# Score matmuls of a chunked linear-attention kernel: from two 64-column strips of the array to four of 32

## The chip, the cores and the metric

The kernel runs on one core of one Trainium2 chip. A core has a matrix engine (TensorE, PE in the profile; its weight loads are listed apart as PEld), a vector engine (VectorE, DVE), a scalar engine (ScalarE, ACT), a general one (GpSimd, POOL), a queue engine (SyncE, SP) and 16 DMA engines. Matmul results land in PSUM, eight banks of 2 KB per partition; everything else on the chip lies in SBUF. The metric is the device time of one execution in microseconds, lower is better; the time of a kernel is the median of its runs.

## The reference, cut to what matters

Two blocks follow each other. The first is a gated linear recurrence, per batch and head, over 768 tokens with head size 48; the second puts its output through four experts and adds them up with weights.

```python
# batch 4, heads 8, tokens S = 768, head size 48
for t in range(S):
    state = alpha[:, :, t, :, None] * state + np.einsum('bhd,bhe->bhde', k[:, :, t], v[:, :, t])
    y[:, :, t] = np.einsum('bhd,bhde->bhe', q[:, :, t], state)
x = y.transpose(0, 2, 1, 3).reshape(3072, 384)
p = domain_probs / (domain_probs.sum(-1, keepdims=True) + 1e-09)
for e in range(4):                       # w1[e]: 384 x 1024, w2[e]: 1024 x 384
    out += p[:, e:e + 1] * (np.maximum(x @ w1[e], 0.0) @ w2[e])
```

All of it is float32.

## The kernel before, in words

**Units.** The tokens are cut into chunks of 128. A unit is one chunk of one batch, 24 in all (6 chunks x 4 batches). Its eight heads lie in four pairs; a head is padded from 48 to 64 rows, so that a pair fills the 128 rows of the array. A unit makes the output of its 128 tokens out of the state that the chunk before left, and out of the products of its own keys and queries.

**Levels.** A key s and a later query t of one chunk get a score that carries the gates between them. The kernel orders the pairs (s, t) by the size at which they part in a binary tree over the 128 tokens: at level m (1, 2, 4, ... 64; `LEVELS`, index li 0 to 6) the keys are the lower halves and the queries the upper halves of blocks of 2m tokens. Query and key tiles are multiplied by gates from one level to the next (`next_q`, line 490, `next_k`, line 499); `copy_q` (line 480) copies the 64 queries of the upper halves into a tile `qb` in which the two heads of a pair stand side by side, each in its own 64 rows, with zeros elsewhere. `qb` has four buffers, handed round by the deque `free`.

**Scores.** For levels 1 to 32 (li 0 to 5) `products` (line 509) makes eight matmuls, one for each pair of heads and each half s of the keys: 64 key columns as weights, 2 x 32 query columns streamed, the result in 64 of the 128 PSUM partitions. Two such matmuls, for s = 0 and 1, stand side by side in the array, in two strips of 64 columns. In a half, the result of 64 keys x 32 queries holds all blocks of that half, and only the entries inside a block count. `take` (line 519) picks them out with a mask of 0 and 1: a predicated copy on DVE of 128 x 256 elements (8 heads x 32 queries) into `near`, which has 128 x 8 x 64 elements and starts as a diagonal of the terms with s = t (line 539). Level 64 (li 6) needs no mask: four groups of matmuls (line 569) write `far`, and ACT copies it to its place in `lat` (line 582). Later ACT copies the two 64 x 64 diagonal blocks of `near` into `lat` (line 586), and `result` (line 594) multiplies `lat` by the values and adds the state's part, in four strips of 32 columns (line 608).

**PSUM.** Score tiles have the tag "sc" with two buffers of one bank. Levels 0 to 3 take two tiles of two levels each (line 542), levels 4 and 5 a third (line 564), `far` a fourth.

**Precision.** These matmuls are plain float32: the profile lists each as two records of matmul and two of weight load. The matmuls of the experts are float32r (one record), three of them for each product, because operands are split into a rounded and a rest part; only the first group of units runs them in plain float32.

**The order of the work.** Everything that PE does is issued in the order of the program; PE executes it in that order, except that matmuls in different strips of the array go on side by side. The experts' matmuls (`up`, line 660; `down`, line 723) carry the program. `attention(u)` (line 422) is a generator with 17 steps, parted by `yield`; `deal` (line 810) gives each step of each unit a due time on a clock that counts only the experts' work (`cost`, line 804), and `advance` (line 858) runs the due steps between two of the experts' matmuls. Steps counted from 0: 0 to 2 turn alpha, k, q; 3 to 5 do levels 0 to 2 of `copy_q`, `next_q`, `next_k`; 6 copies level 3 and sets up `near`; 7 issues the products of levels 0 to 3 together and takes levels 0 and 1; 8 takes levels 2 and 3; 9 and 10 prepare levels 5 and 6; 11 issues the products of levels 64, 16 and 32 together and takes levels 16 and 32; 12 copies `far`; 13 copies the diagonal of `near`; 14 and 15 turn the keys and make the result; 16 renews the state. Two units are under way at a time, and for many units step 7 is put right behind step 15 of the unit before (`TOGETHER`, line 131). The first unit has a function of its own (`first_unit`, line 239), with matmuls of 64 rows x 64 columns and 32 streamed columns in four tiles of the array at once (line 295).

Of the kernel before, what the change touches and what calls it, by code (L numbers as in the profile page):

```python
# [20 lines left out]
def kernel(  # L21
# [35 lines left out]
    mask_np = np.concatenate([mask_np.reshape(P, -1), j == np.arange(HALF)[None, :]], 1).astype(np.uint8)  # L57
    used = (np.arange(P)[:, None] % HD < D)
    ident_np = np.concatenate([np.eye(P), np.tile(np.eye(HALF), (2, 1)), used], 1).astype(np.float32)
# [8 lines left out]
    ident_all = const.tile([P, P + HALF + 1], F32, name="ident")  # L68
    ident = ident_all[:, :P]
    masks_all = const.tile([P, 6 * QUAD + HALF], U8, name="masks")  # L70
    masks = masks_all[:, :6 * QUAD].rearrange("p (l n) -> p l n", n=QUAD)
    NBLK = B * NCB
    p_all = const.tile([P, NBLK, E], F32, name="p_all")
    tot = const.tile([P, NBLK], F32, name="tot")

    near = const.tile([P, H, HALF], F32, name="near")
    lat = const.tile([P, H, P], F32, name="lat")

    sts = [const.tile([P, NP, 2, D], F32, name=f"st{b}") for b in range(B)]
# [30 lines left out]
    free = deque(blocks)  # L110
# [128 lines left out]
    def first_unit(fill, other):  # L239
# [17 lines left out]
        rows = [slice(HD * i, HD * (i + 1)) for i in range(2)]  # L257
# [44 lines left out]
        def take(li, outs):  # L302
            for i in range(2):
                to = diag[:, NP * i:NP * (i + 1)]
                if li < 0:
                    nc.vector.copy_predicated(
                        to, masks_all[:, 6 * QUAD:].unsqueeze(1).broadcast_to([P, NP, HALF]), outs[i])
# [114 lines left out]
    def attention(u):  # L422
        cb, b = units[u]
# [18 lines left out]
        yield  # L442
        KT = keys()
        if u >= in_runs:
            nc.scalar.activation(out=AT, in_=AT, func=ACT.Copy, scale=ident_all[:, P + HALF:])  # L445
            turn("k", KT)
        else:
            nc.scalar.copy(out=KT, in_=turned(pair(rk)))
# [50 lines left out]
        def next_k(li):  # L499
            m = LEVELS[li]  # L500
            old = new = halves(KTs[li], m)
            if li + 1 < len(LEVELS):
# [3 lines left out]
            nc.vector.tensor_mul(new[:, :, :, 0, :], old[:, :, :, 0, :],  # L506
                                 spread(halved(decs[li])[:, :, :, 1], m))

        def products(li, out):

            for p in range(NP):
                for s in range(2):
                    nc.tensor.matmul(  # L513
                        out[HALF * s:HALF * (s + 1), 2 * p:2 * p + 2, :],
                        lhsT=KTs[li][:, p, HALF * s:HALF * (s + 1)],
                        rhs=qbs[li][:, p, :, QUAD * s:QUAD * (s + 1)], start=True, stop=True)
            free.append(qbs[li])

        def take(li, scores):
            m = LEVELS[li]  # L520
            nb = HALF // (2 * m)
            mk = masks[:, li, :].rearrange("p (b r) -> p b r", r=m)
            nc.vector.copy_predicated(  # L523
                near.rearrange("p a (b two r) -> p a b two r", two=2, r=m)[:, :, :, 1, :],
                mk.unsqueeze(1).broadcast_to([P, H, nb, m]),
                scores.rearrange("p a (b r) -> p a b r", r=m))

        def scores():
            return ps.tile([P, 2, H, QUAD], F32, name="sc", tag="sc")


        for li in range(3):
# [3 lines left out]
            yield  # L536
        copy_q(3)

        nc.vector.tensor_mul(near, ident_all[:, P:P + HALF].unsqueeze(1).broadcast_to([P, H, HALF]),
                             dot.unsqueeze(2).broadcast_to([P, H, HALF]))  # L540
        yield
        banks = [scores() for _ in range(2)]
        for li in range(4):
            products(li, banks[li // 2][:, li % 2])
        next_q(3)
        next_k(3)
        take(0, banks[0][:, 0])
        take(1, banks[0][:, 1])
        yield
        copy_q(4)  # L550
        next_q(4)
        next_k(4)
        take(2, banks[1][:, 0])
        take(3, banks[1][:, 1])
        yield
        copy_q(5)
        next_q(5)
# [4 lines left out]
            next_q(6)  # L562
        yield
        bank = scores()
        far = ps.tile([P, NP // 2, 2, HALF], F32, name="far", tag="sc")

        for r in range(NP // 2):
            for s in range(2):
                nc.tensor.matmul(far[HALF * s:HALF * (s + 1), r],  # L569
                                 lhsT=KTs[6][:, 2 * r + s, :HALF], rhs=qbs[6][:, 2 * r + s],  # L570
                                 start=True, stop=True)
        for li in (4, 5):
            products(li, bank[:, li - 4])
        free.append(qbs[6])
        take(4, bank[:, 0])
        take(5, bank[:, 1])
        next_k(6)
        yield
        parts = lat.rearrange("p (r s i) c -> p r s i c", s=2, i=2)
        for s in range(2):  # L580
            rows = slice(HALF * s, HALF * (s + 1))
            nc.scalar.copy(out=parts[:HALF, :, s, :, HALF:], in_=far[rows])
        yield
        for s in range(2):
            rows = slice(HALF * s, HALF * (s + 1))
            nc.scalar.copy(out=lat[rows, :, rows], in_=near[rows])
        KT = KTs[-1]
        yield
# [275 lines left out]
    with tc.manual_schedule():  # L864
        nc.scalar.dma_start(out=ident_all, in_=nc.inline_tensor(ident_np, name="ident_c").ap())
        nc.scalar.dma_start(out=masks_all, in_=nc.inline_tensor(mask_np, name="masks_c").ap())
        nc.gpsimd.memset(sts[B - 1], 0.0)
        for nm in "akq":
            for r in (early[nm], apart[nm]):
                nc.gpsimd.memset(r[:, :, D:], 0.0)  # L870
        nc.gpsimd.memset(lat[HALF:, :, :HALF], 0.0)
        for t in values + blocks:
            nc.gpsimd.memset(t, 0.0)
        for t in sts[:-1]:
            nc.gpsimd.memset(t, 0.0)
# [72 lines left out]
```

## Time and profile before

| what | value |
|---|---|
| median of 3 runs | 1011.13 us (1010.61 to 1011.39) |
| the profiled execution's own time | 1010.73 us |
| its span in the trace | 1009.0 us |
| PE matmul busy | 994.1 us, 99% |
| PE weight load busy | 885.8 us, 88% |
| DVE busy | 547.0 us, 54% |
| ACT busy | 426.0 us, 42% |
| POOL busy | 36.1 us, 4% |
| granted PE clock | 1.0 |
| score matmuls, line 513 | 2208 records, 73.7 us busy |
| predicated copies, line 523 | 138 of 128 x 256, 536 ns each |

A line of the profile names the line of the kernel, the engine, the operation, the tiles (out<-in), the shape and a count; "128*64 128x64" at a matmul means 128 rows and 64 columns of the array in use and 64 columns streamed. Busy time is the union of the records, so that overlapping matmuls are not counted twice; the mean of one record is its latency, not the pace at which records follow each other. "Issue" as a reason for idle time means that the profile shows nothing that the engine waited for.

### The profile page before, as it was taken

The page shows a single profiled execution, that of the slowest core. Times are in us where ns is not written, and L with a number is a line of the kernel's source. Part 1 is how long each engine was busy: PE and PEld are TensorE (multiplying, and loading weights), DVE is VectorE, ACT ScalarE, POOL GpSimd, SP SyncE. Part 2 cuts the span into 40 slices and gives each one's busy share as a digit, 9 for nine tenths or more (in the row PEclk, how much of TensorE's full clock was granted, in tenths as well). Part 3 has the DMA queues.
Part 4 walks back from the last instruction along what each step waited for, and adds up shares of the span by engine and source line. Part 5 has one row for each costly group of instructions (what it writes and reads, how often), then busy time and mean ns, then how long its engine had stood idle before and what let it go on. Part 6 is the DMA issues. An engine that isn't in the chain of part 4 may idle for free.

```text
span 1009.0 us, 20864 instructions
## 1 busy us (share of the span) xinstructions
PE 994.1 (99%) x8564; PEld 885.8 (88%) x8564; DVE 547.0 (54%) x1178; ACT 426.0 (42%) x936; POOL 36.1 (4%) x79
## 2 busy tenths in 40 slices
PE   8899999999999999999999999999999999999998
PEld 7777778988988889889899899898898989999998
DVE  5677757366676555666645645756676521222222
ACT  5786666354463552533533514445443432111111
POOL 2000001000000000000000000000000000000000
PEclk9999999999999999999999999999999999999999
DMA  9696788284776683854945828748656405151511
GB/s 210 220 291 201 239 285 306 71 325 118 269 228 210 216 232 124 276 196 150 316 146 178 293 100 247 252 123 277 218 159 253 155 8 196 55 206 45 206 60 32
DMA packets 155118, 194.12 MB, mean 192 GB/s; under 512 B 95216, under 2 KB 131440, under 8 KB 155024
## 3 DMA queue, kind: packets, MB, share of 16 engines
q1 hardware_dynamic: 148560, 162.97, 51.2%
q0 software_dynamic: 6016, 29.49, 7.5%
q8 instruction: 68, 1.11, 0.5%
q10 hardware_dynamic: 448, 0.33, 0.1%
q14 instruction: 26, 0.21, 0.1%
HBM read 162.87 MB, written 29.88 MB: 191 GB/s over the span
## 4 chain that ended last, share of the span: by engine, by line
PE 92%; DVE 3%; ACT 3%; issue 1%; DMA 1%; SPq 0%; DVEq 0%; ACTq 0%
PE ops L764 40%; PE one L695 35%; PE sc L513 6%; PE yps L608 3%; PE one L689 3%; PE tp L236 2%; PE sps L639 1%; PE far L569 1%; ACT qb L487 1%; DVE w L210 1%; DMA sk<-in_k_dram 1%; DVE near L523 1%; DMA w<-kept 0%; ACT KT L505 0%; DVE QT L494 0%
## 5 line engine op out<-in xcount | busy, mean ns | idle before, releaser
L764 PE MATMUL ops<-w,hT 128*128 128x384 f32 x2112 | 380.6, 338 | 0.1
L764 PEld LDWEIGHTS ops<-w,hT 128*128 128x128 f32 x2112 | 364.4, 188 | 4.0 <-issue 0.8
L695 PE MATMUL one<-xT,w 128*128 128x512 f32 x1440 | 340.4, 394 | 0.0
L695 PEld LDWEIGHTS one<-xT,w 128*128 128x128 f32 x1440 | 268.3, 188 | 56.9
L697 ACT ACTIVATE hT<-one 128x512 fp32r<-128x512 f32 (+1 forms) x192 | 108.0, 562 | 302.5 <-PE one L695 301.7
L720 DVE SCALAR_TENSOR_TENSOR hT<-one,hT 128x512 fp32r<-128x512 f32 (+1 forms) x192 | 121.8, 642 | 117.5 <-ACT hT L697 117.4
L487 ACT COPY qb<-QT 64x256 f32<-64x256 f32 x322 | 131.2, 407 | 68.0 <-DVE QT L494 36.4
L494 DVE TENSOR_TENSOR QT<-QT,AT 128x256 f32<-128x256 f32 x158 | 66.8, 423 | 103.3 <-ACT qb L487 102.6
L790 DVE SCALAR_TENSOR_TENSOR acc<-ops,p_all,acc 128x384 f32<-128x384 f32 x66 | 38.1, 612 | 91.8 <-PE ops L764 91.8
L523 DVE COPY_PREDICATED near<-masks,sc 128x256 f32<-128x256 uint8 x138 | 74.0, 536 | 20.6 <-PE sc L513 18.1
L513 PEld LDWEIGHTS sc<-qb,KT 128*64 128x64 f32 x2208 | 69.5, 138 | 7.0 <-issue 5.3
L513 PE MATMUL sc<-qb,KT 128*64 128x64 f32 x2208 | 73.7, 223 | 1.3 <-ACT qb L487 1.2
L506 DVE TENSOR_TENSOR KT<-KT,AT 128x256 f32<-128x256 f32 x161 | 67.2, 418 | 3.1 <-PE tp L236 3.1
L505 ACT COPY KT<-KT 128x256 f32<-128x256 f32 x138 | 57.5, 417 | 3.4
L689 PE MATMUL one<-xT,raw 128*128 128x256 f32 (+1 forms) x240 | 46.0, 340 | 0.4 <-ACT xT L406 0.4
L764 PE MATMUL ops<-raw,hT 128*128 128x384 f32 x128 | 45.5, 492 | 0.0
L689 PEld LDWEIGHTS one<-xT,raw 128*128 128x128 f32 x240 | 37.9, 191 | 4.9 <-ACT xT L406 0.6
L496 DVE TENSOR_TENSOR AT<-AT 128x256 f32<-128x256 f32 (+1 forms) x138 | 39.2, 284 | 4.7
L799 POOL DMA_DIRECT2D out_dram<-acc x22 | 11.8, 541 | 680.2 <-DVE acc L790 680.2
L445 ACT ACTIVATE AT<-AT,ident 128x512 f32<-128x512 f32 x14 | 10.2, 726 | 60.8 <-DVE AT L434 59.9
L695 PE MATMUL one<-raw,w 128*128 128x256 f32 x288 | 34.6, 279 | 0.0
L695 PEld LDWEIGHTS one<-raw,w 128*128 128x128 f32 x288 | 34.4, 188 | 0.0
(110 smaller groups left out, 631.6 us busy)
## 6 DMA issues: line engine op xcount, KB each, us to landing
w<-kept SPq DMA_DIRECT2D x144, 768.0 KB, 7.2
kept<-w POOLq DMA_DIRECT2D x32, 768.0 KB, 6.3
raw<-in_moe_w_dram SPq DMA_DIRECT2D x48, 384.0 KB, 6.7
rv<-in_v_dram SPq DMA_DIRECT2D x24, 192.0 KB, 2.9
out_dram<-acc POOLq DMA_DIRECT2D x22, 192.0 KB, 2.4
rk<-in_k_dram SPq DMA_DIRECT2D x14, 192.0 KB, 3.2
rq<-in_q_dram SPq DMA_DIRECT2D x14, 192.0 KB, 8.6
sa<-in_alpha_dram SPq DMA_DIRECT2D x28, 88.0 KB, 2.1
```

What stands on the lines that cost most here:

```text
L487: nc.scalar.copy(out=qb[rows, :, i, :].rearrange("p a (b r) -> p a b r", r=m), in_=qv[rows])
L494: nc.vector.tensor_mul(qv, qv, spread(dv[:, :, :, 0], m))
L496: nc.vector.tensor_mul(dec, dv[:, :, :, 0], dv[:, :, :, 1])
L505: nc.scalar.copy(out=new[:, :, :, 1, :], in_=old[:, :, :, 1, :])
L506: nc.vector.tensor_mul(new[:, :, :, 0, :], old[:, :, :, 0, :], spread(halved(decs[li])[:, :, :, 1], m))
L513: nc.tensor.matmul(out[HALF * s:HALF * (s + 1), 2 * p:2 * p + 2, :], lhsT=KTs[li][:, p, HALF * s:HALF * (s + 1)], rhs=qbs[li][:, p, :, QUA ...
L523: nc.vector.copy_predicated(near.rearrange("p a (b two r) -> p a b two r", two=2, r=m)[:, :, :, 1, :], mk.unsqueeze(1).broadcast_to([P, H, ...
L689: nc.tensor.matmul(one, lhsT=w[:, kc], rhs=xTs[gi][:, 0, kc, lo:hi], start=(kc == 0), stop=(kc == KC - 1))
L695: nc.tensor.matmul(one, lhsT=w[:, of_w, kc], rhs=x_part(gi, of_x)[:, kc, :n], start=k == 0, stop=k == len(turns) - 1)
L697: nc.scalar.activation(out=parts[0], in_=one, func=ACT.Relu)
L720: nc.vector.scalar_tensor_tensor(out=low, in0=x, scalar=0.0, in1=top.bitcast(F32), op0=ALU.max, op1=ALU.subtract)
L764: nc.tensor.matmul(sums[slot], lhsT=h, rhs=w, start=(n == begins[slot]), stop=(n == ends[slot]))
```

## The change

Levels 1 to 16 (li 0 to 4) go from two strips of 64 keys to four strips of 32: a level is now 16 matmuls with 32 weight columns and 2 x 16 streamed columns, in place of eight with 64 and 2 x 32. `near` shrinks from 64 to 32 columns per head, the masks (`strip_masks`) and the copies of `take` from 32 to 16 queries per head. Four levels fit in one bank, so step 7 takes one score tile and step 11 one.

Level 32 (li 5) leaves `products` and `take`: inside a half of 64 tokens it is one full block of 32 keys x 32 queries, so it needs no mask. Its eight matmuls use 32 weight columns each; a strip is given to one half s of one of two pairs of heads (`odd`), so that two pairs are done at once. ACT copies the result from PSUM into `lat` in four pieces, in step 12, behind the two copies of `far`. `cross` and `far` are parts of the bank that holds level 16. In step 11 the order is now level 64, level 16, level 32. In step 13 the diagonal is copied in four pieces of 32 x 32 per head in place of two of 64 x 64. All of `lat` is zeroed at the start, in place of a quarter.

```diff
+    NSTRIP = P // QUAD
+    HQ = QUAD // 2
+    strip_np = np.stack([(js // (2 * m) == n[:, :HQ] // m) & (js % (2 * m) < m) for m in LEVELS[:5]], 1)
...
-    near = const.tile([P, H, HALF], F32, name="near")
+    near = const.tile([P, H, QUAD], F32, name="near")
...
+        strips = [slice(QUAD * j, QUAD * (j + 1)) for j in range(NSTRIP)]
+
         def products(li, out):
-
             for p in range(NP):
-                for s in range(2):
-                    nc.tensor.matmul(
-                        out[HALF * s:HALF * (s + 1), 2 * p:2 * p + 2, :],
-                        lhsT=KTs[li][:, p, HALF * s:HALF * (s + 1)],
-                        rhs=qbs[li][:, p, :, QUAD * s:QUAD * (s + 1)], start=True, stop=True)
+                for j, rows in enumerate(strips):
+                    nc.tensor.matmul(out[rows, 2 * p:2 * p + 2, :], lhsT=KTs[li][:, p, rows],
+                                     rhs=qbs[li][:, p, :, HQ * j:HQ * (j + 1)], start=True, stop=True)
             free.append(qbs[li])
...
         def scores():
-            return ps.tile([P, 2, H, QUAD], F32, name="sc", tag="sc")
+            return ps.tile([P, 4, H, HQ], F32, name="sc", tag="sc")
...
-        banks = [scores() for _ in range(2)]
+        bank = scores()
         for li in range(4):
-            products(li, banks[li // 2][:, li % 2])
+            products(li, bank[:, li])
...
         bank = scores()
-        far = ps.tile([P, NP // 2, 2, HALF], F32, name="far", tag="sc")
-
+        cross = bank[:, 1].rearrange("p a n -> p (a n)").rearrange("p (r i n) -> p r i n", r=NP // 2, i=2)
+        far = bank[:, 2:].rearrange("p l a n -> p (l a n)").rearrange("p (r i n) -> p r i n", r=NP // 2, i=2)
...
-        for li in (4, 5):
-            products(li, bank[:, li - 4])
         free.append(qbs[6])
+        products(4, bank[:, 0])
+        for r in range(NP // 2):
+            for j, rows in enumerate(strips):
+                odd, s = divmod(j, 2)
+                nc.tensor.matmul(cross[rows, r], lhsT=KTs[5][:, 2 * r + odd, strips[2 * s]],
+                                 rhs=qbs[5][:, 2 * r + odd, :, QUAD * s:QUAD * (s + 1)], start=True, stop=True)
+        free.append(qbs[5])
         take(4, bank[:, 0])
-        take(5, bank[:, 1])
         next_k(6)
         yield
...
             nc.scalar.copy(out=parts[:HALF, :, s, :, HALF:], in_=far[rows])
-        yield
-        for s in range(2):
-            rows = slice(HALF * s, HALF * (s + 1))
+        for j, rows in enumerate(strips):
+            odd, s = divmod(j, 2)
+            nc.scalar.copy(out=parts[strips[2 * s], :, odd, :, strips[2 * s + 1]], in_=cross[rows])
+        yield
+        for rows in strips:
             nc.scalar.copy(out=lat[rows, :, rows], in_=near[rows])
...
-        nc.gpsimd.memset(lat[HALF:, :, :HALF], 0.0)
+        nc.gpsimd.memset(lat, 0.0)
```

More of the change, by code (lines that the diff above doesn't have):

```diff
@@ L57 @@
     mask_np = np.concatenate([mask_np.reshape(P, -1), j == np.arange(HALF)[None, :]], 1).astype(np.uint8)
+    NSTRIP = P // QUAD
+    HQ = QUAD // 2
+    js = np.arange(P)[:, None] % QUAD
+    strip_np = np.stack([(js // (2 * m) == n[:, :HQ] // m) & (js % (2 * m) < m) for m in LEVELS[:5]], 1)
+    mask_np = np.concatenate([mask_np, strip_np.reshape(P, -1)], 1).astype(np.uint8)
     used = (np.arange(P)[:, None] % HD < D)
-    ident_np = np.concatenate([np.eye(P), np.tile(np.eye(HALF), (2, 1)), used], 1).astype(np.float32)
+    ident_np = np.concatenate([np.eye(P), np.tile(np.eye(QUAD), (NSTRIP, 1)), used], 1).astype(np.float32)
     const = ctx.enter_context(tc.tile_pool(name="const", bufs=1))
@@ L66 @@
     ps = ctx.enter_context(tc.tile_pool(name="ps", bufs=2, space=bass.MemoryType.PSUM))
-    ident_all = const.tile([P, P + HALF + 1], F32, name="ident")
+    ident_all = const.tile([P, P + QUAD + 1], F32, name="ident")
     ident = ident_all[:, :P]
-    masks_all = const.tile([P, 6 * QUAD + HALF], U8, name="masks")
+    masks_all = const.tile([P, 6 * QUAD + HALF + 5 * HQ], U8, name="masks")
     masks = masks_all[:, :6 * QUAD].rearrange("p (l n) -> p l n", n=QUAD)
+    same = masks_all[:, 6 * QUAD:6 * QUAD + HALF]
+    strip_masks = masks_all[:, 6 * QUAD + HALF:].rearrange("p (l n) -> p l n", n=HQ)
     NBLK = B * NCB
@@ L306, in take @@
                     nc.vector.copy_predicated(
-                        to, masks_all[:, 6 * QUAD:].unsqueeze(1).broadcast_to([P, NP, HALF]), outs[i])
+                        to, same.unsqueeze(1).broadcast_to([P, NP, HALF]), outs[i])
                     continue
@@ L444, in attention @@
         if u >= in_runs:
-            nc.scalar.activation(out=AT, in_=AT, func=ACT.Copy, scale=ident_all[:, P + HALF:])
+            nc.scalar.activation(out=AT, in_=AT, func=ACT.Copy, scale=ident_all[:, P + QUAD:])
             turn("k", KT)
@@ L520, in take @@
             m = LEVELS[li]
-            nb = HALF // (2 * m)
-            mk = masks[:, li, :].rearrange("p (b r) -> p b r", r=m)
+            nb = QUAD // (2 * m)
+            mk = strip_masks[:, li, :].rearrange("p (b r) -> p b r", r=m)
             nc.vector.copy_predicated(
@@ L537, in attention @@
         copy_q(3)
-        nc.vector.tensor_mul(near, ident_all[:, P:P + HALF].unsqueeze(1).broadcast_to([P, H, HALF]),
-                             dot.unsqueeze(2).broadcast_to([P, H, HALF]))
+        nc.vector.tensor_mul(near, ident_all[:, P:P + QUAD].unsqueeze(1).broadcast_to([P, H, QUAD]),
+                             dot.unsqueeze(2).broadcast_to([P, H, QUAD]))
         yield
-        banks = [scores() for _ in range(2)]
+        bank = scores()
         for li in range(4):
-            products(li, banks[li // 2][:, li % 2])
+            products(li, bank[:, li])
         next_q(3)
         next_k(3)
-        take(0, banks[0][:, 0])
-        take(1, banks[0][:, 1])
+        take(0, bank[:, 0])
+        take(1, bank[:, 1])
         yield
@@ L552, in attention @@
         next_k(4)
-        take(2, banks[1][:, 0])
-        take(3, banks[1][:, 1])
+        take(2, bank[:, 2])
+        take(3, bank[:, 3])
         yield
```

## The prediction

> **What bounds the kernel now.** First the engines' shares and the chain that ended last, then the stretches, then the rows of the score matmuls.
>
> ```profile
> PE 994.1 (99%) x8564; PEld 885.8 (88%) x8564; DVE 547.0 (54%) x1178; ACT 426.0 (42%) x936; POOL 36.1 (4%) x79
> ...
> PE 92%; DVE 3%; ACT 3%; issue 1%; DMA 1%; SPq 0%; DVEq 0%; ACTq 0%
> PE ops L764 40%; PE one L695 35%; PE sc L513 6%; PE yps L608 3%; PE one L689 3%; PE tp L236 2%; PE sps L639 1%; PE far L569 1%; ACT qb L487 1%; DVE w L210 1%; DMA sk<-in_k_dram 1%; DVE near L523 1%; DMA w<-kept 0%; ACT KT L505 0%; DVE QT L494 0%
> ```
>
> PE is the bound, and the score matmuls (L513) are 6% of the chain. By stretches (columns: stretch, its length, busy time of each engine with its records, clock, DMA share, GB/s):
>
> ```profile
> 20.00:130.00 110.00, 104.64 (x1071) 83.14 (x1072) 75.08 (x173) 78.13 (x186) 7.59 (x14) 1.00 0.74 232
> 130.00:350.00 220.00, 219.04 (x1912) 191.68 (x1912) 138.41 (x297) 109.36 (x233) 13.27 (x27) 1.00 0.68 232
> 350.00:620.00 270.00, 270.00 (x2342) 242.85 (x2340) 154.65 (x326) 108.88 (x235) 2.14 (x4) 1.00 0.64 205
> 620.00:830.00 210.00, 210.00 (x1873) 189.56 (x1873) 126.41 (x272) 91.30 (x202) 4.30 (x8) 1.00 0.56 181
> ```
>
> From 130 us to 830 us PE has no idle time worth naming, DVE and ACT are half idle, and the DMA engines have room. So PE time taken out there shortens the span one for one; before 130 us some of it is lost to waits. One unit's score matmuls, in the timeline of PE alone (start, time to the last end, line, records):
>
> ```profile
> 379.26 0.40 PE L608 MATMUL yps<-lat,rv 128*32 128x128 f32 x8
> 379.59 2.08 PE L513 MATMUL sc<-qb,KT 128*64 128x64 f32 x64
> 381.61 0.45 PE L764 MATMUL ops<-w,hT 128*128 128x384 f32 x1
> ...
> 394.11 0.62 PE L569 MATMUL far<-qb,KT 128*64 128x128 f32 x8
> 394.56 1.10 PE L513 MATMUL sc<-qb,KT 128*64 128x64 f32 x32
> 395.59 0.45 PE L764 MATMUL ops<-w,hT 128*128 128x384 f32 x1
> ```
>
> From its first matmul to the next line's first, levels 0 to 3 take 2.015 us and levels 4 and 5 1.031 us, 3.05 us a unit, 70 us for 23 units (the first has its own function, untouched).
>
> **The pace of small matmuls.** In the trace's single starts the records of one strip follow each other every 58.3 ns in L513, with the other strip 6.6 ns beside it. Which side sets this?
>
> ```profile
> L639 PE MATMUL sps<-rv,AT x208: 222/243/275, 44.5 to 704.2; 128*64 128x48 f32 x56, 128*128 128x96 f32 x48
> ...
> L404 PE MATMUL y<-w,rv x64: 216/219/243, 17.7 to 20.1; 64*32 64x64 f32 x32, 128*32 128x64 f32 x32
> ...
> L295 PE MATMUL sc<-w,w x96: 186/219/240, 9.8 to 16.3; 64*64 64x32 f32 x96
> ```
>
> With 64 weight columns the step is 58.3 ns for 32 (L295), 48 (L639) and 64 streamed columns alike; with 128 weight columns and 96 streamed it is 111.7 ns (L639's other form); with 32 weight columns and 64 streamed it falls to 55.9 ns (L404), with 128 streamed to 109 ns (L608). So the weight load sets it at 64 and 128 columns, 53.4 ns per 64: at 32 columns 58.3 - 26.7 = 31.6 ns. The stream sets L404 and L608, 53.1 ns per 64 columns: at 32 columns 55.9 - 26.6 = 29.3 ns. The later holds: 31.6 ns for a record in each of four strips, 7.9 ns a record. That is an extrapolation; no row has 32 weight columns with 32 streamed. Its support: at a burst's start, L608's second load in a strip begins 29 ns after the first, L513's 55 ns.
>
> The queue must deliver one record per 7.9 ns. Usually it runs some 16 records ahead; where it had run dry (46.3 us) it passed 20 records in 151 ns, 7.6 each, and at 70.2 us 12 in 88 ns, 7.3 each. That just suffices. The 51 ns semaphore events, two a unit at L513, are covered now by 16 records at 29 ns; then by 16 at 7.9, 126 ns. I put 0.05 us a unit on them.
>
> **PE, part by part.** Levels 0 to 3: 64 matmuls are 128 records, 32 groups of four at 31.6 ns, 1.01 us, plus 0.14 us of ends (now 0.15 us): 1.15 us for 2.015, -0.865. Level 4: 8 groups, 0.25 us. Level 5: 8 matmuls are 16 records with 64 streamed columns, four groups at L404's 55.9 ns, 0.22 us. Ends 0.15 us. L569 before them has 64-column strips, and a change of strip width drains the array: from L608 (32) to L513 (64) the last start to the next first is 203 ns, against 109 within L608; that is 0.1 us more here. Sum 0.72 for 1.031, -0.31. Where L608 stands right before levels 0 to 3, 15 times, the drain goes away: 15 x 0.094 = -1.4 us.
>
> Unit 1 (29 to 40 us) I count at nothing: there the chain runs over ACT and DVE (L487, L494, L523), so what PE saves becomes waiting. Beside it DVE gets shorter by four takes and `near`, about 0.9 us, and ACT longer by up to 1.5 us before the result; net between -1 and +1 us, taken as 0. Sum: 22 x (0.865 + 0.31 - 0.05) + 1.4 = 26.1 us off.
>
> **DVE.** Per unit six copies of 536 ns become five of 128 x 128. L311 has that shape, 382 ns (scores) and 274 ns: 1.9 us at the dearer for 3.2. Setting up `near`, 682 ns at 128 x 512, becomes about 423 ns (L494's 128 x 256). That is 1.6 us less, 36 us in all, hidden under PE: no gain, no cost.
>
> **ACT.** Two copies of 64 x 512 at 616 ns become four of 32 x 256, between 363 (L582) and 407 ns (L487): 1.23 to 1.6 us. Four copies of 32 x 128 are added, nearest L271's 128 x 128 at 298 ns: 1.2 us. Some 1.5 us more a unit, 35 us in all, ACT at 46%. In step 12 six copies hold ACT about 1.9 us instead of 0.73. Queued behind them are the experts' relu (L697) and the other unit's `qb` copies; who waits then is PE, for a score or hidden tile. The relu's tile has three more buffers, each some 2 us of PE; steps lie 3 us or more apart. I take 0; uncovered, it is up to 35 us.
>
> **PSUM.** One tile a step instead of two: step 11 no longer holds both buffers. I take 0; the nearest waits, DVE for L513, are not PE's.
>
> **Start and DMA.** POOL's zeroing of `lat` quadruples in area: 523 ns for 64 x 512 is about 1.05 us for 128 x 1024. The value tile (L873) behind it is what SP waits for at 3.31 us; all of SP's later loads move by 0.5 us. Unit 1's alpha would land near 10.1 us and is used at 10.9, the first weights near 16 and 20.7: hidden; uncovered 0.5 us. The instruction queue moved 1.11 MB for 17128 PE records; 3680 more are 0.24 MB, 15 fetches of about 1 us beside the rest. No other queue gets or loses a step.
>
> So 1010.7 - 26.1 = 984.6 us for the profiled execution; it lies 0.4 us under the median, which gives 985.0.
>
> **The rivals.** With r ns a record, a unit's two bursts are 160 r + 591 ns, against 3046 and some 60 of drain.
>
> *The queue does not keep up.* At 7.3 to 7.6 ns the margin is thin. At r = 10 a unit saves 0.91 us, at 12 0.59: 991 to 999 us. Against it are the two catches above; for it, that they are the only ones.
>
> *A 32-column stream costs as much as a 64-column one.* L404's 55.9 ns per four is r = 14.0, L295's 58.3 is 14.6: 0.27 or 0.18 us a unit, 1005 to 1007 us. For it: L295's median latency is 219 ns, L404's with 64 columns too. Against it: the first records of a burst, which wait for their weights, last 240 ns (L295, 32 columns), 257 (L639, 48) and 270 (L513, 64), on a straight line. [...]
>
> [...]
>
> *Slower: ACT's extra copies end on PE.* Place: steps 12 and 13, ahead of the next unit's `qb` copies. Price: 1.5 us x 23 = 35 us against 26 gained, 1019 us; it decides from 1.1 us a unit on PE. For it: at 99.6 us a burst already stands 1.46 us for ACT's `qb`. Against: from 350 to 620 us PE never waits, ACT is 40% busy, and DVE, ahead of it in that chain, gets 1.6 us shorter.
>
> **How the numbers follow.** Chances: the forecast 0.64 (980 to 989: r from 7.3, unit 1 gaining 1 us and no event cost, to 9.3); the queue 0.10; the stream's floor 0.13; no change, r from 15 to 16.4, 0.03; slower 0.10, of it ACT 0.08 and the floor for all strips 0.01. Changes under 0.2% (2 us) can't be told from none, the runs spread by 0.8 us. Faster 0.87, same 0.03, slower 0.10. The range takes the forecast and the queue (0.74) and reaches into the stream's floor: 979 to 1006.
>
> **What would show it.** L513's starts in a strip 31 to 33 ns apart and its first burst 1.1 to 1.2 us long; the second near 0.6 us behind a gap of 0.2; copies of L523's successor under 0.4 us; ACT near 460 us, DVE near 511; PE still at 99% with no new waits for ACT. Starts near 40 ns with short queues mean the queue, near 56 the stream's floor; PE waiting for `qb`, `lat` or hidden tiles means ACT. I am wrong altogether if the strips don't run side by side.

## The result, and the profile after

The changed kernel takes 1021.0 us (median of six runs, 1017.1 to 1025.4), the kernel before, on the same chip, 1011.3 us (1010.6 to 1012.0): a ratio of 1.0093, interval 1.0078 to 1.0108. I had forecast 985 us. It went to the other side.

The profiled execution took 1020.4 us, with a span of 1018.6 us against 1009.0. The page's engine shares and its chain by engine:

```profile
PE 980.0 (96%) x10404; PEld 868.7 (85%) x10404; DVE 509.7 (50%) x1155; ACT 458.0 (45%) x1074; POOL 36.3 (4%) x79
...
PE 91%; ACT 4%; issue 3%; DVE 1%; DVEq 0%; POOL 0%; ACTq 0%; POOLq 0%
```

PE is busy 14.1 us less and the span is 9.6 us longer: PE now idles 38.6 us instead of 14.9, and "issue" has gone from 1% to 3% of the chain. By the same stretches as before:

```profile
20.00:130.00 110.00, 97.12 (x1474) 74.74 (x1463) 67.55 (x166) 79.44 (x199) 7.59 (x14) 0.98 0.74 231
130.00:350.00 220.00, 215.34 (x2352) 187.34 (x2351) 129.38 (x293) 121.20 (x277) 13.26 (x27) 0.99 0.70 233
350.00:620.00 270.00, 261.40 (x2812) 234.82 (x2811) 138.01 (x312) 114.93 (x272) 2.14 (x4) 0.99 0.61 194
620.00:830.00 210.00, 205.40 (x2351) 183.27 (x2350) 123.02 (x276) 101.78 (x240) 4.29 (x8) 1.00 0.64 196
```

Between 130 and 830 us, where PE had hardly stopped (0.96 us in all), it now stands still for 17.9 us, and the granted clock (the third number from the end) is no longer 1.00 everywhere. Yet the bursts themselves did what was forecast. One of them in the timeline of PE (start, time to the last end, line, records):

```profile
426.31 0.40 PE L620 MATMUL yps<-lat,rv 128*32 128x128 f32 x8
426.53 1.37 PE L521 MATMUL sc<-qb,KT 128*32 128x32 f32 x128
427.83 0.61 PE L776 MATMUL ops<-w,hT 128*128 128x384 f32 x2
```

and a second burst:

```profile
402.33 0.46 PE L521 MATMUL sc<-qb,KT 128*32 128x32 f32 x32
402.60 0.45 PE L583 MATMUL sc<-qb,KT 128*32 128x64 f32 x16
402.99 0.44 PE L776 MATMUL ops<-w,hT 128*128 128x384 f32 x1
```

426.53 to 427.83 is 1.30 us for levels 0 to 3, against 2.015. 402.33 to 402.99 is 0.66 us for the second burst; with the drain ahead of it, which is 0.1 us longer than before, it takes 0.76 us, against 1.03. What PE waited for instead, from the list of its waits (total us, times, longest):

```profile
PE sc L521 <- issue: 13.7, 8, 2.9
PE yps L620 <- ACT lat L598: 5.0, 3, 2.5
PE sc L521 <- ACT qb L494: 4.6, 3, 2.0
PE sc L575 <- ACT qb L494: 2.1, 2, 1.5
PE ops L776 <- issue: 1.6, 1, 1.6
PE yps L620 <- issue: 1.5, 1, 1.5
```

The same list of the trace of before has, of these:

```profile
PE far L569 <- ACT qb L487: 2.5, 2, 1.7
...
PE sc L513 <- ACT qb L487: 1.2, 1, 1.2
...
PE yps L608 <- ACT lat L586: 0.5, 2, 0.3
```

There L608 waited 0.5 us for `lat`, the score matmuls 3.7 us for `qb`, and "issue" stood for 1.8 us in all, in two waits of the first unit; no score burst of the later units waited for it. One of the new stalls, in the same kind of timeline, falls inside a burst:

```profile
308.11 0.80 PE L521 MATMUL sc<-qb,KT 128*32 128x32 f32 x64
310.94 0.27 PE L521 MATMUL sc<-qb,KT 128*32 128x32 f32 x8 [2.03 <-issue]
311.14 0.45 PE L776 MATMUL ops<-w,hT 128*128 128x384 f32 x1
```

120 of the 128 records run, then PE waits 2.03 us for nothing that the profile names, then the last eight run. The other loss is the clock. By stretches, two places where the clock was halved:

```profile
344.30:347.70 3.40, 3.40 (x14) 3.30 (x13) 0.29 (x1) 0.88 (x2) 0.00 (x0) 0.50 0.32 127
388.70:392.10 3.40, 3.40 (x12) 3.40 (x12) 2.21 (x9) 2.02 (x5) 0.00 (x0) 0.50 0.04 14
```

The trace's record of the granted clock has five such windows of 3.41 us at 0.50 (at 16.6, 105.4, 344.3, 388.7 and 470.6 us), each behind an idle stretch of PE of 1.5 to 2.9 us, and none in the trace of before, at 1.00 from 5.9 us to the end of its span. PE counts as busy in them. I put each at half its length, 1.7 us; the starts of L776's matmuls, 0.320 us apart in them and 0.174 outside, make it 1.55 us. By the first, 5 x 1.7 = 8.5 us. So the work that PE had to do fell by about 14.1 + 8.5 = 22.6 us, and 23.7 us of idle time and 8.5 us of half clock came on top: +9.6 us.

### The profile page after: what moved, and what is told of

The parts are those of the page before. It is cut to its first block, busy times and chain, and to the rows that moved or that the text cites. A ratio compares the mean times of both kernels' runs of the same rounds, so it can differ in the third digit from the quotient of the medians.

```text
span 1018.6 us, 24660 instructions
## 1 busy us (share of the span) xinstructions
PE 980.0 (96%) x10404; PEld 868.7 (85%) x10404; DVE 509.7 (50%) x1155; ACT 458.0 (45%) x1074; POOL 36.3 (4%) x79
## 4 chain that ended last, share of the span: by engine, by line
PE 91%; ACT 4%; issue 3%; DVE 1%; DVEq 0%; POOL 0%; ACTq 0%; POOLq 0%
PE ops L776 40%; PE one L707 36%; PE sc L521 3%; PE yps L620 3%; PE one L701 3%; PE tp L243 2%; ACT qb L494 1%; PE sps L651 1%; PE sc L575 1%; ACT lat L598 1%; PE sc L583 1%; ACT KT L512 1%; ACT lat L595 0%; PE idle L901 0%; ACT w L215 0%
## 5 line engine op out<-in xcount | busy, mean ns | idle before, releaser
L776 PE MATMUL ops<-w,hT 128*128 128x384 f32 x2112 | 384.7, 341 | 1.6 <-issue 1.6
L776 PEld LDWEIGHTS ops<-w,hT 128*128 128x128 f32 x2112 | 368.4, 190 | 5.2 <-issue 2.5
L521 PE MATMUL sc<-qb,KT 128*32 128x32 f32 x3680 | 44.6, 199 | 18.3 <-issue 13.7
L521 PEld LDWEIGHTS sc<-qb,KT 128*32 128x32 f32 x3680 | 39.7, 110 | 26.1 <-issue 18.1
L529 DVE COPY_PREDICATED near<-masks,sc 128x128 f32<-128x128 uint8 x115 | 40.8, 355 | 28.6 <-PE sc L521 16.4
L776 PE MATMUL ops<-raw,hT 128*128 128x384 f32 x128 | 45.5, 492 | 0.0
L620 PE MATMUL yps<-lat,rv 128*32 128x128 f32 x736 | 33.8, 273 | 6.5 <-ACT lat L598 5.0
L598 ACT COPY lat<-near 32x256 f32<-32x256 f32 x92 | 36.9, 401 | 0.8
L620 PEld LDWEIGHTS yps<-lat,rv 128*32 128x32 f32 x736 | 29.3, 110 | 8.6 <-ACT lat L598 6.7
```

What stands on the lines that cost most here:

```text
L521: nc.tensor.matmul(out[rows, 2 * p:2 * p + 2, :], lhsT=KTs[li][:, p, rows], rhs=qbs[li][:, p, :, HQ * j:HQ * (j + 1)], start=True, stop=True)
L620: nc.tensor.matmul(yps[QUAD * j:QUAD * (j + 1), c, :], lhsT=lhsT, rhs=rhs, start=begins, stop=ends)
L776: nc.tensor.matmul(sums[slot], lhsT=h, rhs=w, start=(n == begins[slot]), stop=(n == ends[slot]))
```

## Where the stalls lie

I counted PE's records in the order of time, as the trace has them: weight loads, matmuls and the semaphore events between them. Then I looked up each step of over 0.7 us between two matmul records inside a group. Start of the step, its length, the record it stands before, and that record's place in the count, whole and modulo 256:

```
kernel after                                            place  mod 256
 14.03  1.73 us  before record  16 of  29, line 302       448  192
 78.36  0.82 us  before record  96 of 128, line 521      2288  240
102.33  2.09 us  before record  96 of 128, line 521      2889   73
125.25  1.79 us  before record  30 of  56, line 620      3521  193
308.72  2.23 us  before record 120 of 128, line 521      7616  192
340.43  2.25 us  before record  96 of 128, line 521      8210   18
384.92  2.23 us  before record  76 of 128, line 521      9152  192
466.12  3.10 us  before record 109 of 128, line 521     10945  193
550.54  1.91 us  before record  14 of  68, line 776     12736  192
588.02  2.29 us  before record  95 of 128, line 521     13504  192
675.10  1.24 us  before record  93 of 128, line 521     15296  192
708.63  2.25 us  before record  93 of 128, line 521     16065  193
743.18  1.40 us  before record  85 of 128, line 521     16833  193
```

The three at 240, 73 and 18 stand before record 96, where level 8 begins; these are the waits for ACT's `qb`. The ten others stand before a different record each time, but always at 192 or 193 of a count that runs over at 256. An eleventh, of 0.3 us at 807 us, has this place too. The kernel before has it at two waits, of 0.7 and 1.1 us at 15 and 20 us, both in the first unit. Of all that is called "issue" in the kernel after, 18.7 us, only one wait of 0.4 us, at 86 us, stands elsewhere (102).

I take the queue that the profile lists as "q8 instruction" to be the one that brings PE's instructions: it moved 82 pieces of 16,384 bytes in the kernel after, with 21,039 records so counted, and 68 in the kernel before, with 17,367, so one piece for some 256 records. From the DMA view of the changed kernel, first 306.0 to 308.7 us, then 308.7 to 311.0 us (packets, MB, share of the 16 engines):

```profile
q1 hardware_dynamic: 120, 0.65, 57.3%
q0 software_dynamic: 78, 0.38, 33.9%
```

```profile
q8 instruction: 1, 0.02, 2.5%
q1 hardware_dynamic: 1, 0.00, 0.0%
```

I take it that a border between two pieces lies where the stalls are. Then the border before this one was passed at 306.4 us. Until 308.7 us q8 moves nothing, while the other queues fill the engines to nine tenths (57.3% and 33.9%); then one piece comes, at 308.74 us, in 0.93 us; 1.27 us later PE goes on. At another stall (708.6 us) border, fetch and end of the stall lie at 706.7, 708.5 and 710.9 us. At the ten stalls of the table the piece starts to come 0.5 to 3.5 us after the border before, and PE goes on 3.1 to 5.8 us after that border, each time 1.2 to 1.6 us after the piece has landed. In the changed kernel L620 and the first burst, which often stand together, use 368 instructions in 2.85 us; in the one before it was 240 in 3.7 us. From border to border the 256 records lasted 1.7 to 2.3 us at eight of the ten stalls, 3.6 and 4.0 us at the other two. At four more borders they lasted 2.0 to 4.5 us and PE did not stall; there the piece had landed 1.5 us or more before it was needed. In the trace of before they never last less than 5.0 us after the first unit.

## The experiments

Three theories, numbered as in the expectations. Theory 1: PE runs out of instructions at the borders of these pieces, because the new bursts use them too fast. Theory 2: one bank for four levels; PE's writes and DVE's reads of the same bank get into each other's way. Theory 3: ACT's added copies, the slower rival of the prediction.

**The burst cut in two (e1_split).** The kernel after, with levels 4 and 8 issued one step later:

```diff
-        for li in range(4):
+        for li in range(2):
             products(li, bank[:, li])
...
         yield
+        for li in (2, 3):
+            products(li, bank[:, li])
         copy_q(4)
```

> The changed kernel with the products of levels 4 and 8 (li 2 and 3) issued in step 8 instead of step 7; same matmuls, same bank, same copies. Theory 1, PE runs out of instructions: one block of 256 PE instructions is fetched while the one before is used up, and needs some 3.5 to 5 us; the dense run of line 620 plus levels 1 to 8 (112 + 256 instructions in 2.85 us) falls to 112 + 128 in about 2.2 us, so that 256 instructions take at least 3.8 us. Then at most 3 stalls near 2 us are left of 11, the clock stays at 1.0 after 30 us, and the time is 989 to 995 us (the gain of some 24 us less 0.2 us of further drain a unit). Theory 2, PE's writes and DVE's reads in one bank get in each other's way, or a wait among the engines: the same stalls, in one burst or the other, 1012 to 1021 us. Theory 3, ACT's longer copies are what PE waits for: 1012 to 1021 us.

Measured: 1008.66 us, ratio 0.9968 (0.9955 to 0.9981). Waits of PE:

```profile
PE sc L521 <- DVE near L529: 7.8, 3, 3.9
PE yps L622 <- ACT lat L600: 5.0, 3, 2.5
PE sc L521 <- issue: 1.8, 2, 1.1
```

The stalls on "issue" in L521 fall from 13.7 to 1.8 us, with the same matmuls. Two things kept the time above what theory 1 gave: ACT's `lat`, 5.0 us as in the kernel after, and a wait that this edit made itself, 7.8 us in which the second half of the burst, in the same tile, waits until DVE has read the first. Half-clock windows begin at 82.6 and 109.9 us, behind two of these waits.

**Two tiles for the four levels (e2_two_banks).** The kernel after, with as many score tiles in step 7 as before:

```diff
-        bank = scores()
+        banks = [scores() for _ in range(2)]
         for li in range(4):
-            products(li, bank[:, li])
+            products(li, banks[li // 2][:, li % 2])
```

> The changed kernel with levels 1 and 2 in one bank and levels 4 and 8 in another, as the kernel before had them; the burst of 128 records stays whole. Theory 1 (instructions run out): nothing changes, 1017 to 1023 us, about 10 stalls near 2 us in the first burst. Theory 2 (one bank for four levels): the stalls go, 985 to 995 us.

Measured: 1020.84 us, 1.0087 (1.0061 to 1.0113), as the kernel after. Its waits:

```profile
PE sc L521 <- issue: 11.9, 6, 2.5
PE yps L620 <- ACT lat L598: 5.0, 3, 2.5
```

Theory 2 falls for the first burst.

**Level 32 alone (e3_level32).** The kernel before, with its first burst untouched; level 32 in four strips, its four ACT copies, and the diagonal in four copies:

```diff
-        for li in (4, 5):
-            products(li, bank[:, li - 4])
+        products(4, bank[:, 0])
+        for r in range(NP // 2):
+            for j, rows in enumerate(strips):
+                odd, s = divmod(j, 2)
+                nc.tensor.matmul(cross[rows, r], lhsT=KTs[5][:, 2 * r + odd, strips[2 * s]],
+                                 rhs=qbs[5][:, 2 * r + odd, :, QUAD * s:QUAD * (s + 1)], start=True, stop=True)
...
+        for j, rows in enumerate(strips):
+            odd, s = divmod(j, 2)
+            nc.scalar.copy(out=parts[strips[2 * s], :, odd, :, strips[2 * s + 1]], in_=cross[rows])
```

> The kernel before, with only level 32 changed: four strips, two pairs of heads at once, four copies from PSUM on ACT, diagonal copied in four pieces, one predicated copy less on DVE; levels 1 to 16 stay in two strips. It has ACT's 1.5 us more a unit but no more PE instructions than before. Theory 1 (instructions run out): no stalls, the second burst about 0.1 us shorter a unit, 1007 to 1011 us. Theory 3 (ACT's copies end on PE): most of the loss is here too, over 1014 us.

Measured: 1015.55 us, 1.0036 (1.0022 to 1.0049). Its waits:

```profile
PE yps L617 <- ACT lat L595: 4.4, 3, 1.9
PE sc L513 <- ACT qb L487: 2.7, 2, 1.5
PE far L569 <- ACT qb L487: 2.6, 2, 1.7
```

No stall at a border after the first unit (there one of 0.9 us), but 4.4 us for `lat` and 5.3 for `qb`, against 0.5 and 3.7 before. So theory 1 is not the whole of it: level 32 with ACT's copies is by itself a loss of about 4 us, where theory 1 alone had 1007 to 1011 us.

**More instructions, the old bursts (e4_filler).** The kernel before, with 32 tiny matmuls ahead of step 7's products (128 instructions a unit; their results are overwritten):

```diff
+        for p in range(NP):
+            for k in range(2):
+                for j in range(P // QUAD):
+                    rows = slice(QUAD * j, QUAD * (j + 1))
+                    nc.tensor.matmul(banks[1][rows, 1, 2 * p:2 * p + 2, 0], lhsT=KTs[0][:, p, rows],
+                                     rhs=qbs[0][:, p, :, k], start=True, stop=True)
```

> The kernel before, with 32 small matmuls (32 weight columns, 2 streamed) put in front of the products of levels 1 to 8 in every unit; their results are overwritten by the products behind them. They make 128 PE instructions more, 0.5 to 0.7 us of array a unit, 12 to 16 us in all; nothing else changes. Theory 1 (instructions run out): stalls near 2 us called issue in about 8 to 12 bursts, the clock halved after some of them, 1035 to 1055 us. Theories 2 and 3: no stalls, 1022 to 1028 us.

Measured: 1036.82 us (two runs), 1.0247 (1.0226 to 1.0267). The wait that matters:

```profile
PE sc L513 <- issue: 8.3, 5, 2.4
```

Four stalls of 1.6 to 2.4 us appear in the old, wide bursts (389, 433, 556 and 600 us), at places 192 and 193 modulo 256. Fewer than expected, but the kernel before has none in these bursts: here 128 more instructions a unit were enough, whatever the strips, tiles and copies. The rest of the added time is the fillers' own work: PE is busy 19.4 us more, of which three half-clock windows (17.2, 392.7 and 559.9 us) make 5.1.

**Separate tiles, and DVE instead of ACT (e5_tiles, e6_dve).** e5 is e1 with a tile for each half of the burst and one for `far`; e6, the second diff, is e5 with level 32 copied by DVE:

```diff
-        bank = scores()
+        banks = [scores()]
...
+        banks.append(scores())
+        for li in (2, 3):
+            products(li, banks[1][:, li])
...
+        far = ps.tile([P, NP // 2, 2, HALF], F32, name="far", tag="sc")
```

```diff
-            nc.scalar.copy(out=parts[strips[2 * s], :, odd, :, strips[2 * s + 1]], in_=cross[rows])
+            nc.vector.tensor_copy(out=parts[strips[2 * s], :, odd, :, strips[2 * s + 1]], in_=cross[rows])
```

> The split version (levels 4 and 8 in step 8) with tiles of their own for the two halves of levels 1 to 8, and for the scores of level 64. In the split version PE waits 7.8 us in three places for DVE's copies out of the same tile, and ACT's copy of level 64 waits for DVE's copy of level 16. If these waits come from sharing the tile, they go: PE's waits for DVE's predicated copies fall under 1 us, and the time falls by 5 to 9 us against the split version, to 1000 to 1004 us. If they come from DVE being late, the time stays at 1006 to 1010 us.

> The version with tiles of their own, and the four copies of level 32 on DVE instead of ACT. Theory: in the first 130 us ACT is the late engine, and its four extra copies a unit are what the result (line 620) waits for there, 5.0 us in three places. Then these waits fall under 2 us, and the time by another 3 to 5 us, to 996 to 1001 us. If ACT's copies are covered, no change against the version before.

Measured: e5 998.54 us, 0.9879 (0.9848 to 0.991); e6 994.58 us, 0.9833 (0.9818 to 0.9848), both 1.4 us below what I had expected. The profiled execution of e5, 1003.85 us, had a granted clock of 0.95 from end to end; without it the median of e5 is 997.5 us. The shares of e6 and three of PE's waits, from its page and its list:

```profile
PE 977.1 (98%) x10404; PEld 861.2 (87%) x10404; DVE 534.7 (54%) x1247; ACT 434.2 (44%) x982; POOL 36.3 (4%) x79
```

```profile
PE far L578 <- ACT qb L494: 1.3, 1, 1.3
...
PE sc L521 <- issue: 1.2, 1, 1.2
...
PE yps L623 <- ACT lat L601: 1.1, 2, 0.7
```

PE's wait for DVE is gone with the shared tile (e5), and the waits for `lat`, 3.8 us in e5, fall to 1.1 us when 24 us of copies move from ACT to DVE (e6). e6 does the same matmuls as the kernel after and is the fastest kernel of this study, 17 us under the one before.

**Apart in time (e7_apart, e8_after_apart).** One rule in `deal`: where step 7 falls together with step 15 of the unit before, it comes 2.5 us later. e7 has it on e6, e8 on the kernel after, whose burst stays whole:

```diff
+                if times[:-1] and abs(times[-1][7] - times[-2][15]) < 2.5:
+                    times[-1][7] = times[-2][15] + 2.5
```

> The version with the copies on DVE, and step 7 put 2.5 us of expert work behind the result of the unit before wherever the two fell together (15 times); one line in deal. The dense run of 240 PE instructions becomes 112 and 128. Theory 1 (instructions run out): the last stalls called issue in the score bursts, three of some 3 us in all, go; the drains between strips cost 15 x 0.2 = 3 us, so the time is within 3 us of the version before it, and the spread of the runs is smaller, because the halved clock behind stalls goes too.

> The changed kernel, whole burst of 128 records, one bank, ACT's copies as they are; only step 7 put 2.5 us of expert work behind the result where the two fell together. The dense run falls from 368 PE instructions to 256, and two block borders 256 apart hardly fit in it. Theory 1 (instructions run out): 2 to 5 stalls in the first bursts instead of 11, the time 1004 to 1012 us. Theory 2 (something in the burst itself): 10 or more stalls as before, 1019 to 1026 us.

Measured: e7 997.23 us, 0.9861 (0.9846 to 0.9876), so on the split burst the rule costs 2.6 us; the gap where strips change width comes back (268 ns from the last start to the first, instead of 89). The spread of its runs is 1.9 us, against 1.1 in e6; I had expected it to be smaller. e8 1003.27 us, 0.9925 (0.9907 to 0.9943), 0.7 us below the range that I gave for theory 1, against 1021.0 without the rule. Waits of e8:

```profile
PE yps L620 <- ACT lat L598: 5.1, 3, 2.5
PE sc L521 <- issue: 2.6, 2, 1.7
```

With the burst, its tile and ACT's copies unchanged, distance alone takes away 11 of the 13.7 us of "issue", and 17.7 us of time. Not all of that is theory 1: in the profiled execution the waits for `qb` are 2.8 us shorter too, and there are two half-clock windows instead of five.

**The borders moved (e9_shift).** The kernel after with 32 tiny matmuls, 128 instructions, at the very start, so that each border falls half a piece earlier in the program:

```diff
+        for n in range(32):
+            j = n % NSTRIP * QUAD
+            nc.tensor.matmul(idle[j:j + QUAD, :2], lhsT=zeros[:, j:j + QUAD], rhs=zeros[:, :2],
+                             start=True, stop=True)
```

> The changed kernel with 32 tiny matmuls more at its very start, among the ones that keep the array busy while the first inputs arrive: 128 PE instructions, half a microsecond once. Nothing of the work behind them changes, but every border between blocks of 256 PE instructions falls half a block earlier in the program. Theory 1 (instructions run out at a border, when the block before was used up in under some 3 us): counted through the program, the stalls after 200 us move to other bursts: to those that ran at 269, 343, 427, 508 and 547 us, and away from those at 308, 384, 465, 587, 674, 708 and 742 us; five instead of ten, the time 1004 to 1013 us. Theory 2 (anything that belongs to the bursts themselves: the bank, waits, ACT): the same bursts stall, and the time stays at 1019 to 1024 us.

Measured: 1017.44 us, 1.006 (1.0042 to 1.0077). By the same count as above:

```
kernel e9_shift                                         place  mod 256
268.58  2.51 us  before record  91 of 128, line 521      6849  193
339.50  2.25 us  before record  96 of 128, line 521      8338  146
386.49  2.19 us  before record  12 of  68, line 776      9409  193
426.25  2.65 us  before record  93 of 128, line 521     10177  193
507.94  4.04 us  before record 125 of 128, line 521     11968  192
551.69  2.43 us  before record  79 of 128, line 521     12737  193
```

The bursts that stalled at 308, 466, 588, 675, 708 and 743 us now run through, others stall in their place, and again at 192 or 193. Of the five that I had named, four do (269, 427, 508 and 547 us), the one at 343 us does not. The wait for `qb` at 340 us stayed with its record, and its place moved by 128, from 18 to 146. This is the plainest evidence for theory 1. The time is above what I expected: after 260 us the stalls are five instead of eight, but longer, 12.7 us in all, and five windows of half clock remain.

**ACT relieved, the burst whole (e10_act).** The kernel after, with `far` in its own tile and level 32 copied by DVE:

```diff
-        far = bank[:, 2:].rearrange("p l a n -> p (l a n)").rearrange("p (r i n) -> p r i n", r=NP // 2, i=2)
+        far = ps.tile([P, NP // 2, 2, HALF], F32, name="far", tag="sc")
...
-            nc.scalar.copy(out=parts[strips[2 * s], :, odd, :, strips[2 * s + 1]], in_=cross[rows])
+            nc.vector.tensor_copy(out=parts[strips[2 * s], :, odd, :, strips[2 * s + 1]], in_=cross[rows])
```

> The changed kernel, whole burst, with two edits for ACT alone: the four copies of level 32 on DVE, and level 64 in a tile of its own, so that ACT's copy of it doesn't wait for DVE's copy of level 16. Theory: this takes away the 5.0 us that PE waits for the result's operand in the first 130 us, and little else, while the stalls at block borders stay: 1011 to 1017 us. If ACT's copies cost nothing there, 1019 to 1023 us.

Measured: 1007.22 us (1004.8 to 1013.6), 0.9961 (0.9941 to 0.9982), 3.8 us below the range that I gave. Waits of its profiled execution, at 1013.6 us its longest:

```profile
PE sc L521 <- issue: 12.0, 7, 2.8
PE sc L521 <- ACT qb L494: 3.1, 3, 1.9
PE far L575 <- ACT qb L494: 2.1, 2, 1.5
```

The stalls on "issue" stay, `lat` is down to 1.2 us, and the half-clock window at 344 us is not there; four others are. Between the two profiled executions these differences, with 1.5 us less for `qb`, are about 7 us, and the spans are 6.8 us apart. The gain of 13.8 us in the medians is more than that; the clock seems to be a part of it. The mean clock of its seven runs lies between 0.992 and 0.998, 0.997 in the median run, against 0.991 in the profiled run of the kernel after: 0.006 of 1010 us is 6 us. Why fewer stalls meet a half-clock window here stays open.

## Why the prediction was wrong

**PE's work: right, and a little too high.** Loads in a strip follow each other every 31.7 ns in the first groups of a burst (said: 31.6), but from the sixth group on a record comes every 8.3 ns, not 7.9. The first burst measured 1.30 us for 1.20 with events, so 0.1 x 22 = 2.2 us less; the second, with its drain, 0.756 for 0.72. The drains went as said: L569's successor takes 0.588 us instead of 0.488, and the gap from L620 to L521 is 89 ns instead of 203. Of 26.1 us, about 22.6 came. One floor under the starts of all strips, which has 0.01 in the chances, is shown by no run: four strips side by side went at 8.3 ns a record in the kernel after.

**"15 fetches of about 1 us beside the rest": the step that failed.** The number of fetches (82 for 68, so 14 more) and their length were about right. Counting a fetch by its bytes was the error. What counted was when it landed: at the ten stalls PE went on 1.2 to 1.6 us after the piece had landed, and at the four borders without a stall the piece had landed 1.5 us or more before it was needed. A burst that ran 1.5 times as fast (1.30 us for 2.015) through twice as many instructions (256 for 128) came to the next border sooner. The waits at the borders cost 18.3 us, 14.9 of them in eight stalls after 300 us, against 1.8 us in the kernel before, and two half-clock windows behind them 3.4 us. The row I used to show that PE's queue can deliver 7.3 to 7.6 ns a record was one of 20 records; it said nothing of the supply of the next 256. The rival "the queue does not keep up" had the place, but priced only the pace, at 991 to 999 us.

**"I take 0" for ACT: wrong, and the rival half right.** ACT's copies as such were sized well: 458.0 us in all for a forecast of 460, 256 and 401 ns each. But they were not covered. The timeline of all engines of the changed kernel shows the rival's mechanism at work at 340 us (lines of ACT and PE):

```profile
337.95 1.06 ACT L595 COPY lat<-sc 32x128 f32<-32x128 f32 x4
...
339.53 1.63 ACT L598 COPY lat<-near 32x256 f32<-32x256 f32 x4
...
341.80 0.82 ACT L494 COPY qb<-QT 64x256 f32<-64x256 f32 x2
...
342.67 0.46 PE L521 MATMUL sc<-qb,KT 128*32 128x32 f32 x32 [2.05 <-ACT qb L494]
```

The four copies of level 32 and the four of the diagonal stand ahead of the `qb` copies, and PE waits 2.05 us for these; a half-clock window follows. In all, PE waits 4.5 us more for `lat` and 3.0 us more for `qb`, and the windows at 105 and 344 us, both behind a wait for `qb`, add 3.4: 10.9 us. I had excluded this by the stretch from 350 to 620 us, where it indeed does not happen; it happens around 100 us, where PE had waited before too, and at 340 us. The rival's time, 1019 us, is near the result by chance: it put 35 us on ACT alone.

**The sum.** 22.6 us of work saved; 19.9 us lost at the borders (16.5 more of waits and the two windows behind them), 10.9 to ACT, 0.4 to the "issue" wait at 86 us, 1.7 to the half-clock window at 16.6 us; the remaining -0.7 us are small waits that went away. That is +9.6 us. The window at 16.6 us lies in the first unit, which the change leaves alone, behind a border wait that the kernel before has too, 1.5 us here and 0.7 there; the traces of e2, e3, e4, e6, e7 and e8 have a window at 15.9 to 17.2 us as well. That these 1.7 us come from the change is not shown.

**"PSUM: I take 0": wrong in a place that costs little as it stands.** DVE and ACT wait for one shared tile in step 11 (ACT's copy of `far` 5.7 us for DVE in all); it is of weight only when the burst is cut, 7.8 us on PE in e1.

**DVE** went as said: 509.7 us for 511, copies of 355 ns within 274 to 382, all of it hidden. It was the place where level 32 should have stayed: e5 to e6 gains 4.0 us in the medians, 3.0 without e5's execution at a clock of 0.95.

What stays open: what delays a fetch after its border (from the border to the fetch the DMA engines' share was 0.92 or more at seven of the eight stalls after 300 us, 0.16 at the one of 675 us, which was seen and not tried), the "issue" wait at 86 us, and why fewer waits met a half-clock window in e10. Padding each unit so that no border falls into a burst was not tried, nor was the whole burst with DVE's copies and the rule of e7.

## What to carry to other kernels

The smaller matmuls cost more instructions here (20,808 matmul and load records for 17,128), these came in pieces of some 256 (82 pieces for 21,039 records, semaphore events counted), and at the ten stalls PE went on only 3.1 to 5.8 us after the border before: before a burst is made denser, count how many instructions PE goes through in any 4 to 5 us, the burst's neighbours included, and put distance between two dense groups. PE time saved is only gained if nothing else becomes late: when PE passes a stretch faster, whatever another engine prepares for the next step has that much less time (PE's waits for ACT's `lat` went from 0.5 to 5.0 us here), so the work that such an engine is given in exchange should be put on the one that nobody waits for (24 us of copies moved from ACT to DVE gave 4.0 us between e5 and e6). And the idle gap of 2.05 us on PE at 340 us cost some 3.7 by my estimate, with half of the 3.41 us window at 344 us behind it.

## What was new about the hardware

- In the kernel after, the queue that I take to bring PE's instructions moved 82 pieces of 16,384 bytes for 21,039 records, in the one before 68 for 17,367. At the ten stalls in the table of the kernel after, 256 records had been used up in 1.7 to 4.0 us; PE then stood still for 1.0 to 2.9 us and went on 1.2 to 1.6 us after the next piece had landed. The place in the count was 192 or 193 modulo 256 each time, as at the border stalls of the kernel before, e4 and e9.
- In the kernel after, a matmul of 32 weight columns and 32 streamed columns, with its load, went every 31.7 ns in one strip in the first groups of a burst, and four strips side by side went at 8.3 ns a record from the sixth group on, 4.2 ns an instruction.
- In the kernel after, waits of PE of 1.5 to 2.9 us were followed in some cases, and not in others of the same length, by 3.41 us at a granted clock of 0.50 (behind the 2.03 us from 385.1 us yes, behind the 2.03 us from 308.9 us no). Which waits are followed by such a window was not shown. The runs of one kernel differ in their mean clock: those of the kernel after go from 1017.1 us at 0.995 to 1025.4 us at 0.988.
